# Feature transform in two row tiles, PV in four column tiles, and a new order in an attention, Fourier and feed-forward kernel

## The chip, the cores and the metric

The kernel runs on one core of a Trainium2 chip. The metric is the device time of one execution in microseconds, and the median over runs is compared. The core has TensorE (matmuls, PE in the profile, its weight loads PEld), VectorE (DVE), ScalarE (ACT), GpSimd (POOL) and SyncE (SP), which issues nearly all DMAs here.

## The reference

Inputs are q, k, v of 4 batches, 12 heads, 448 positions and 64 features each, all f32, and two feed-forward weights of 768 x 3072 and 3072 x 768.

```python
scores = scale * np.matmul(q, k.transpose(0, 1, 3, 2))      # causal mask, softmax
attn_out = np.matmul(attn, v)                                # heads side by side: x is (4, 448, 768)
X = np.fft.fft(np.fft.fft(x, axis=1), axis=2)
u = x + np.real(X)
un = (u - mu) / np.sqrt(var + 1e-06)                         # over the 768 features
return u + np.maximum(un @ w_ch1, 0.0) @ w_ch2
```

## The kernel before

Each step of the program is a unit: a small function, the engine that it runs on, what it reads and writes. Four tables in the code fix everything about the units: RUN is the order in which all of them are emitted, BY the engine of each (P for TensorE, V, S, G, and D for a DMA), BANK the PSUM bank and BUF the buffer. The costs that stand beside the units (SC_COST, D1_COST and the like) went into these tables and are not used at run time. Every engine works through its own units in the order of RUN.

Attention (`attend`, lines 539 to 690) goes by pairs of heads, 6 pairs for each batch, 24 in all. Per pair:
- The queries are scaled into qs (L568 on VectorE or GpSimd, L566 on ScalarE).
- The scores are made in three units. Row blocks 0 and 1 share one, row block 2 has another; in both the two heads lie in the two halves of the 128 rows, so that a matmul has 64 rows (L600, and L593 for the mask, bf16 matmuls that add a large number where a key is masked). The third unit is the tail, both heads in one matmul of 128 rows. The masks come first in all three.
- Minimum (L613, VectorE), exponential with its sum (L621, ScalarE), and normalization of seven blocks p (L651 ScalarE, L653 VectorE, L655 GpSimd).
- 16 transposes in four units (L667, f32), copied out of PSUM to pa.
- PV (L677): for each of seven parts and each head one f32 matmul with 64 weight columns, so that the two heads fill two column tiles and the 128 output partitions are the features of two heads. Then two copies to xt, feature by position.

When a pair and its partner three places on are done, `fold` (lines 691 to 717) makes sums and differences of features and of positions, in f0, f1 and f2. `dft` (lines 719 to 842) runs once per batch: per parity of the position and for cosine and sine (nm is a or b) it multiplies by the feature table cd, in two units of three f32 matmuls each, one for the even and one for the odd frequencies, 194 and 192 columns (L735). This is the first step of the transform. Its result is copied to y (ya, yb), multiplied by the position table cs (L752), and added to x (transposes of xt at L778, sums at L788); means and variances, the normalization (L821, L818) and transposes back (L831) follow, and the result goes to DRAM.

The feed-forward part follows: `f1` (L1034) and `window` (L1204), matmuls in f32r on blocks that are split into high and low halves by ScalarE, VectorE and GpSimd. Its first units fill gaps from batch 2's attention on; from some 230 us it runs alone.

At the start, `warm` (lines 491 to 503) runs 11 matmuls on zeros, `consts` (505 to 524) loads identity and mask in f32 and casts them to bf16 (bfc, on VectorE and GpSimd), and the first pair's queries and keys come in four pieces, all issued by SP.

## Time and profile before

| | us |
|---|---|
| median of 3 runs | 850.25 (850.23 to 851.16) |
| the profiled execution | 849.51 |
| its span, first to last instruction | 847.7 |

Shares of the span that the engines are busy: TensorE 99%, its weight loads 89%, VectorE 84%, ScalarE 66%, GpSimd 56%. The profile is one execution. Starts of matmuls are recorded, their ends modelled, and a matmul's recorded duration contains its way through the array: matmuls that follow one another overlap in it. So the distance from one start to the next is what an instruction costs, and the busy share tells only that TensorE never stood for long. A f32 matmul is recorded as two passes, each with its weight load; f32r and bf16 matmuls as one. The chain leads back from the last instruction to what released each step, and merges neighbours of one line. Merged timeline rows run from the first start to the last end.

### The profile page before, as it was taken

What the parts mean: (1) busy time and instruction counts of PE and PEld (TensorE: products, weight loads), DVE (VectorE), ACT (ScalarE), POOL (GpSimd) and SP (SyncE); (2) the same over time, 40 slices, a digit from 0 to 9 for tenths busy, and PEclk for the clock granted to TensorE, in tenths of its full rate; (3) what the DMA queues carried; (4) which work ended last, traced back from release to release, by engine and by line L of the source; (5) the groups of instructions that cost most, each with busy time, mean ns of one, the idle gap of its engine ahead of it and who ended that gap; (6) DMA issues with size and microseconds to landing.
All of it is one profiled execution on the core that took longest, in us unless ns stands there. A gap on an engine that the chain in (4) does not pass through costs nothing.

```text
span 847.7 us, 15801 instructions
## 1 busy us (share of the span) xinstructions
PE 840.2 (99%) x5407; PEld 755.7 (89%) x5407; DVE 711.7 (84%) x1300; ACT 556.2 (66%) x1148; POOL 472.9 (56%) x509
## 2 busy tenths in 40 slices
...
GB/s 270 203 73 201 226 159 237 245 174 165 232 256 212 232 252 298 284 255 255 265 262 250 263 244 235 186 194 208 94 186 188 145 308 143 113 183 143 131 140 102
DMA packets 121792, 174.03 MB, mean 205 GB/s; under 512 B 21744, under 2 KB 98800, under 8 KB 121712
## 3 DMA queue, kind: packets, MB, share of 16 engines
...
## 4 chain that ended last, share of the span: by engine, by line
PE 90%; DVE 4%; DMA 2%; ACT 2%; issue 1%; POOL 0%; SPq 0%; DVEq 0%; ACTq 0%
PE psum L1204 35%; PE psum L1034 31%; PE psum L600 6%; PE psum L677 5%; PE psum L667 5%; PE psum L735 3%; PE psum L593 1%; PE psum L752 1%; PE psum L778 1%; PE psum L831 1%; DMA raw<-in_qk_dram 1%; DMA us<-und 1%; DVE w L896 1%; DMA w<-in_w_dram 0%; DVE us L902 0%
## 5 line engine op out<-in xcount | busy, mean ns | idle before, releaser
L1204 PE MATMUL psum<-wa,w 128*128 128x384 f32 x1050 | 208.3, 336 | 0.0
L1204 PEld LDWEIGHTS psum<-wa,w 128*128 128x128 f32 x1050 | 184.1, 188 | 0.9 <-DVE w L896 0.2
L1204 PE MATMUL psum<-wb,w 128*128 128x384 f32 x714 | 149.7, 337 | 0.2
L1204 PEld LDWEIGHTS psum<-wb,w 128*128 128x128 f32 x714 | 125.8, 188 | 1.3 <-issue 0.4
L1034 PE MATMUL psum<-0t,w 128*128 128x448 f32 x432 | 106.3, 366 | 0.0
L1034 PE MATMUL psum<-1t,w 128*128 128x448 f32 x432 | 103.6, 363 | 0.0
L896 POOL TENSOR_TENSOR w<-ws,w 128x384 fp32r<-128x384 f32 x58 | 67.1, 1162 | 59.6 <-ACT w L487 46.2
L870 ACT ACTIVATE w<-w 128x768 int8<-128x768 f32 x48 | 94.5, 1968 | 0.7
L487 ACT CAST w<-us 128x384 fp32r<-128x384 f32 x77 | 38.5, 513 | 80.9 <-PE psum L1204 34.6
L621 ACT ACTIVATE p<-psum,mn 128x256 f32<-128x256 f32 (+3 forms) x168 | 83.5, 530 | 9.9 <-DVE mn L613 9.3
L1034 PEld LDWEIGHTS psum<-1t,w 128*128 128x128 f32 x432 | 80.7, 187 | 6.2 <-ACT c L487 0.4
L1034 PEld LDWEIGHTS psum<-0t,w 128*128 128x128 f32 x432 | 80.1, 188 | 6.4 <-DVE c L1060 0.4
L487 ACT CAST w<-ws 128x384 fp32r<-128x384 f32 x86 | 44.3, 519 | 47.5 <-PE psum L1204 25.9
L1220 DVE TENSOR_TENSOR acc<-psum,acc 128x384 f32<-128x384 f32 x96 | 50.8, 548 | 23.0 <-PE psum L1204 22.8
L613 DVE TENSOR_REDUCE mn<-psum 128x1 f32<-128x448 f32 (+3 forms) x96 | 61.9, 664 | 6.7 <-PE psum L600 5.0
L600 PE MATMUL psum<-raw,qs 64*128 64x384 f32 (+3 forms) x336 | 66.0, 430 | 1.0 <-DVE qs L568 1.0
L896 POOL TENSOR_TENSOR w<-us,w 128x384 fp32r<-128x384 f32 x40 | 46.9, 1175 | 31.1 <-ACT w L487 16.9
L880 DVE SCALAR_TENSOR_TENSOR w<-w,w 128x768 uint32<-128x768 uint32 x48 | 53.0, 1105 | 3.0 <-ACT w L870 2.4
L1034 PE MATMUL psum<-ue,w 128*128 128x448 f32 x216 | 54.3, 367 | 0.3 <-ACT c L1068 0.3
L1060 DVE TENSOR_TENSOR c<-psum,c 128x448 f32<-128x448 f32 x69 | 42.3, 617 | 13.5 <-PE psum L1034 7.9
L667 PEld LDWEIGHTS psum<-cst,p 128*128 128x128 f32 x384 | 42.7, 141 | 11.1 <-issue 3.9
L655 POOL TENSOR_TENSOR p<-p,ri 128x128 f32<-128x128 f32 (+3 forms) x61 | 37.4, 632 | 26.5 <-DVE ri L633 21.5
...
## 6 DMA issues: line engine op xcount, KB each, us to landing
...
```

The costliest lines, as they stand in the source:

```text
L487: nc.scalar.copy(out=out, in_=in_)
L600: nc.tensor.matmul(out=T[ps][:, at[r]:at[r] + n], lhsT=T[qs][s, q0:q0 + 128], rhs=T[raw][s, QW:QW + n], start=False, stop=y == len(rows) - ...
L613: nc.vector.tensor_reduce(out=z, in_=x, axis=AX, op=ALU.min)
L621: nc.scalar.activation(out=T[pb][:, PO[rr]:PO[rr] + n], in_=T[ps][:, c0:c0 + n], func=ACTF.Exp, scale=-1.0, bias=T[mn][:, rr:rr + 1], accu ...
L667: nc.tensor.transpose(T[ps][:, 128 * k:128 * k + 128], T[pb][:, e:e + 128], T["cst", 0][:, 0:128])
L677: nc.tensor.matmul(out=T[xps][64 * h:64 * h + 64, q0:q0 + w], lhsT=T[v][:, c, h * D:(h + 1) * D], rhs=T[pa][:, s0 + h * sd:s0 + h * sd + w ...
L870: nc.scalar.activation(out=T[w].bitcast(I8)[:, :, 3], in_=T[w][:, :, 1].bitcast(F32), func=ACTF.Prelu, scale=SIGN_SCALE, alpha=SIGN_ALPHA)
L880: nc.vector.scalar_tensor_tensor(out=T[w32], in0=T[w32], scalar=3, in1=T[w][:, :, int(join)], op0=ALU.logical_shift_left, op1=ALU.bitwise_or)
L896: (nc.gpsimd if eng == "G" else nc.vector).tensor_tensor(out=lo(), in0=src(), in1=hi(), op=ALU.subtract)
L1034: nc.tensor.matmul(out=T[ps][:, 0:S], lhsT=w[:, a, t], rhs=T[us[t]][:, b], start=first and k == 0, stop=last and k == 8, skip_group_check= ...
L1204: nc.tensor.matmul(out=T[ps][:, 0:384], lhsT=T[hb][:, a, y], rhs=T[z][:, b], start=first and y + v == 0, stop=last and y == n - 1 and v == ...
L1220: nc.vector.tensor_tensor(out=x, in0=T[ps][:, 0:384], in1=x, op=ALU.add)
```

## The change

- The value columns are permuted on the host so that the even features of both heads come first and then the odd ones. PV issues four matmuls of 32 weight columns for each part instead of two of 64, with a tile position each.
- The output partitions of PV therefore hold even features in the lower and odd ones in the upper half. The first step of the transform takes 97 frequencies for each of two table halves (0 to 96 even, 0 to 95 odd) and runs even and odd features as two matmuls of 64 rows, into two PSUM banks. One bank is copied to yt (ScalarE or VectorE), and VectorE makes the frequencies below the middle as a sum and those above as a difference, in mirrored order. The table is half as large. 385 columns of y are used instead of 386, and the sums with x read and write permuted columns.
- Masks: within a row block the mask of 64 columns now comes before that of 128; for row block 2 the scores come first and the masks last.
- Start: 6 warm-up matmuls instead of 11, their memset on GpSimd; the bf16 constants are prepared on the host, so the casts fall away; the first keys and the masks' constants are issued by ScalarE.
- RUN, BY, BANK and BUF are written anew.

```diff
@@ -38,18 +38,18 @@
 BANKS = dict(sc=(1, 3), sd=(1, 2), pt=(1, 3), x=(1, 2), ay=(1, 3), an=(1, 1), at=(1, 5), h0=(0, 4), h1=(0, 4), o2=(0, 8))
-N_P, N_XT, N_Y, N_F, N_D = 3, 1, 1, 1, 1
+N_P, N_XT, N_Y, N_F, N_D, N_YT = 3, 1, 1, 1, 1, 2
 AFTER = dict(E0=("A1",), E2=("A1", "A2"), L=("Q",), F=("E2",), G=("L",))
 BELOW = dict(E2=("E0",))
-C_FROM, W_FROM, N_WARM = 0, 0, 11
+C_FROM, W_FROM, N_WARM = 0, 0, 6
 N_W1, N_C, N_WS = 8, 3, 3
 N_UB, N_US = 4, 4
-SC_COST, TR_COST, PV_COST = (873, 823, 918), 437, 1816
-D1_COST, D2_COST = 977, 650
+SC_COST, TR_COST, PV_COST = (873, 743, 891), 437, 1830
+D1_COST, D2_COST = 585, 650
 BIG = float(2 ** 30)
@@ -87,298 +87,300 @@
 RUN = (
...
 BY = (
...
 BANK = (
...
 BUF = (
...
...
@@ -493,8 +495,8 @@
         def f():
-            nc.vector.memset(T[z][:, 0, 0:256], 0.0)
-        add("V", 200, -4000, f, wr=[(*z, "warm")], phase="A")
+            nc.gpsimd.memset(T[z][:, 0, 0:256], 0.0)
+        add("G", 150, -4000, f, wr=[(*z, "warm")], phase="A")
@@ -503,15 +505,14 @@
     def consts():
-        for key, c0, c1, p in (("b", 128, CW, -2498.5), ("a", 0, 128, -2300)):
-            def f(c0=c0, c1=c1):
-                nc.sync.dma_start(out=T["cst", 0][:, c0:c1], in_=cc[:, c0:c1])
-            add("D", dma(512 * (c1 - c0)), p, f, wr=[("cst", 0, key)], phase="A")
-
-            def f(eng, c0=c0, c1=c1):
-                copy(eng, T["bfc", 0][:, c0:c1], T["cst", 0][:, c0:c1])
-            n = c1 - c0
-            add(("S", "V", "G"), (acts(n), dve(n, 1.92), gps(n)), p + 600, f, rd=[("cst", 0, key)], wr=[("bfc", 0, key)], phase="A")
+        for key, c0, c1, p in (("b", 64, CW // 2, -2498.5), ("a", 0, 64, -2300.5)):
+            def f(c0=c0, c1=c1, first=key == "b"):
+                (nc.scalar if first else nc.sync).dma_start(out=T["bfc", 0].bitcast(F32)[:, c0:c1], in_=cb[:, c0:c1])
+            add("D", dma(512 * (c1 - c0)), p, f, wr=[("bfc", 0, key)], phase="A")
+
+        def f():
+            nc.sync.dma_start(out=T["cst", 0], in_=cc)
+        add("D", dma(65536), -2300, f, wr=[("cst", 0, "a")], phase="A")
...
@@ -541,16 +542,16 @@
-        def load(c0, c1, keys, p):
+        def load(c0, c1, keys, p, second=False):
             def f():
-                nc.sync.dma_start(out=T[raw][:, c0:c1], in_=qk[b, t][:, c0:c1])
+                (nc.scalar if second else nc.sync).dma_start(out=T[raw][:, c0:c1], in_=qk[b, t][:, c0:c1])
             add("D", dma(512 * (c1 - c0)), p, f, wr=keys, phase="A")
         if i == 0:
-            load(QW, QW + 256, [(*raw, "k")], base - 2500)
+            load(QW, QW + 256, [(*raw, "k")], base - 2500, True)
             load(0, 256, [(*raw, "q")], base - 2499)
             load(256, QW, [(*raw, "q1")], base - 2498)
-            load(QW + 256, QW + S, [(*raw, "k1")], base - 2497)
+            load(QW + 256, QW + S, [(*raw, "k1")], base - 2497, True)
         else:
@@ -581,25 +582,23 @@
                 ones, mask = T["bfc", 0][:, 256:CW], T["bfc", 0][:, 128:256]
+                masks, scores = [], []
                 for y, r in enumerate(rows):
-                    e = at[r] + KE[r]
+                    e, n, q0 = at[r] + KE[r], KE[r], 384 if tail else 128 * r
                     if tail:
-                        moves = [(banks[0], e - 64, 64, T["bfc", 0][:, 0:128], mask)]
+                        masks.append((banks[0], e - 64, 64, T["bfc", 0][:, 0:128], mask[:, 0:64]))
                     else:
-                        moves = [
-                            (ps, e - w, w, ones[64 * h:64 * h + 64, a:a + 128], mask[64 * h:64 * h + 64])
-                            for w, a in ((128, 64), (64, 0)) for h, ps in enumerate(banks)]
-                    for z, (ps, c0, w, a, x) in enumerate(moves):
-                        nc.tensor.matmul(
-                            out=T[ps][:, c0:c0 + w], lhsT=a, rhs=x[:, 0:w], start=y == 0 and z < len(banks), stop=False,
-                            skip_group_check=True)
-                for y, r in enumerate(rows):
-                    n, q0 = KE[r], 384 if tail else 128 * r
+                        masks += [
+                            (ps, e - w, w, ones[64 * h:64 * h + 64, a:a + 128], mask[64 * h:64 * h + 64, 0:w])
+                            for w, a in ((64, 0), (128, 64)) for h, ps in enumerate(banks)]
                     for h, ps in enumerate(banks):
                         s = slice(0, 128) if tail else slice(64 * h, 64 * h + 64)
-                        nc.tensor.matmul(
-                            out=T[ps][:, at[r]:at[r] + n], lhsT=T[qs][s, q0:q0 + 128], rhs=T[raw][s, QW:QW + n],
-                            start=False, stop=y == len(rows) - 1, skip_group_check=True)
+                        scores.append((ps, at[r], n, T[qs][s, q0:q0 + 128], T[raw][s, QW:QW + n]))
+                moves = scores + masks if rows == [2] else masks + scores
+                for z, (ps, c0, w, a, x) in enumerate(moves):
+                    nc.tensor.matmul(
+                        out=T[ps][:, c0:c0 + w], lhsT=a, rhs=x, start=z < len(banks), stop=z >= len(moves) - len(banks),
+                        skip_group_check=True)
             add("PE", SC_COST[0 if tail else len(rows)], p0, f, rd=[*([(*qs, 0), (*raw, "k")] if i or k == 0 else [(*qs, 0), (*qs, 1), (*raw, "k"), (*raw, "k1")]), *([(*raw, "k1")] if i else []),
@@ -673,10 +672,11 @@
             for c, q0, w, s0, sd in PARTS:
-                for h in range(2):
+                for z in range(4):
+                    h = z % 2
                     nc.tensor.matmul(
-                        out=T[xps][64 * h:64 * h + 64, q0:q0 + w], lhsT=T[v][:, c, h * D:(h + 1) * D],
-                        rhs=T[pa][:, s0 + h * sd:s0 + h * sd + w], start=q0 + c == 0, stop=c == 3)
+                        out=T[xps][32 * z:32 * z + 32, q0:q0 + w], lhsT=T[v][:, c, 32 * z:32 * z + 32],
+                        rhs=T[pa][:, s0 + h * sd:s0 + h * sd + w], start=q0 + c == 0, stop=c == 3, tile_position=(0, 32 * z))
         add("PE", PV_COST, base + TR_AT + 700, f, rd=[v, *[(*pa, g) for g in range(4)]], wr=[xps], phase="A", mode="C")
@@ -728,21 +728,36 @@
                 mat = 0 if nm == "a" else 1
-                ps = ("ay", (b, par, nm, 1))
-                for dpar, n0, n1 in ((0, 0, 194), (1, 194, 386)):
-                    def f(c0=c0, w=w, mat=mat, ps=ps, dpar=dpar, n0=n0, n1=n1):
+                pe, po = (("ay", (b, par, nm, z)) for z in (1, 3))
+                for dpar in range(2):
+                    def f(c0=c0, w=w, mat=mat, banks=(pe, po), dpar=dpar):
                         for t in range(3):
-                            nc.tensor.matmul(
-                                out=T[ps][0:w, n0:n1], lhsT=T[f"f{t}", (b, t)][:, dpar, c0:c0 + w],
-                                rhs=T["cd", 0][:, mat, t, n0:n1], start=t == 0, stop=t == 2)
+                            for z, ps in enumerate(banks):
+                                s = slice(64 * z, 64 * z + 64)
+                                nc.tensor.matmul(
+                                    out=T[ps][0:w, 97 * dpar:97 * dpar + 97], lhsT=T[f"f{t}", (b, t)][s, dpar, c0:c0 + w],
+                                    rhs=T["cd", 0][s, mat, t, 97 * dpar:97 * dpar + 97], start=t == 0, stop=t == 2)
                     add("PE", D1_COST, nxt(), f, rd=[*[(f"f{t}", (b, t), g) for t in range(3)], ("cd", 0, mat)],
-                        wr=[(*ps, dpar)], phase="Q")
-                y = ("y" + nm, (b, par))
-                rd = [(*ps, 0), (*ps, 1)]
-
-                def f(eng, w=w, ps=ps, y=y):
-                    copy(eng, T[y][0:w], T[ps][0:w, 0:386])
-                add(("S", "V"), (act(386), dve(386)), nxt(), f, rd=rd, wr=[y], phase="Q")
+                        wr=[(*pe, dpar), (*po, dpar)], phase="Q", mode="H")
+                y, yt = ("y" + nm, (b, par)), ("yt", (b, par, nm))
+
+                def f(eng, w=w, po=po, yt=yt):
+                    copy(eng, T[yt][0:w], T[po][0:w, 0:194])
+                add(("S", "V"), (act(194), dve(194)), nxt(), f, rd=[(*po, 0), (*po, 1)], wr=[yt], phase="Q")
+
+                def two(x, w):
+                    return x[0:w].rearrange("p (o c) -> p o c", o=2)
+
+                def f(w=w, pe=pe, yt=yt, y=y, two=two):
+                    nc.vector.tensor_tensor(
+                        out=two(T[y], w)[:, :, 0:97], in0=two(T[pe][:, 0:194], w), in1=two(T[yt], w), op=ALU.add)
+                add("V", dve(194), nxt(), f, rd=[(*pe, 0), (*pe, 1), yt], wr=[(*y, 0)], phase="Q")
+
+                def f(w=w, pe=pe, yt=yt, y=y, two=two, mat=mat):
+                    x = [two(z, w)[:, :, 0:96][:, :, ::-1] for z in (T[pe][:, 0:194], T[yt])]
+                    nc.vector.tensor_tensor(
+                        out=two(T[y][:, 1:385], w)[:, :, 96:192], in0=x[mat], in1=x[1 - mat], op=ALU.subtract)
+                add("V", dve(192), nxt(), f, rd=[(*pe, 0), (*pe, 1), yt, (*y, 0)], wr=[(*y, 1)], phase="Q")
             for nm, g in (("b", 2 + par), ("a", par)):
@@ -750,17 +765,17 @@
                     nc.tensor.matmul(
-                        out=T[ps][0:m, 0:386], lhsT=T["cs", 0][0:k, g, 0:m], rhs=T[y][0:k], start=True, stop=True)
-                add("PE", D2_COST, nxt(), f, rd=[y, ("cs", 0, 0)], wr=[ps], phase="Q")
+                        out=T[ps][0:m, 0:385], lhsT=T["cs", 0][0:k, g, 0:m], rhs=T[y][0:k, 0:385], start=True, stop=True)
+                add("PE", D2_COST, nxt(), f, rd=[(*y, 1), ("cs", 0, 0)], wr=[ps], phase="Q")
                 if nm == "b":
                     def f(eng, m=m, ps=ps, bs=bs):
-                        copy(eng, T[bs][0:m], T[ps][0:m, 0:386])
+                        copy(eng, T[bs][0:m, 0:385], T[ps][0:m, 0:385])
                     add(("S", "V"), (act(386), dve(386)), pr[0] + 1, f, rd=[ps], wr=[bs], phase="Q")
                             nc.vector.tensor_tensor(
-                                out=T[z, (b, par)][0:m, 0:386], in0=T[ps][0:m, 0:386], in1=T[bs][0:m], op=op)
+                                out=T[z, (b, par)][0:m, 0:385], in0=T[ps][0:m, 0:385], in1=T[bs][0:m, 0:385], op=op)
                         add("V", dve(386), pr[0] + 1, f, rd=[ps, bs], wr=[(z, (b, par))], phase="Q")
@@ -781,13 +796,12 @@
                     def f(hf=hf, w=w, ps=ps, key=key, u=u):
-                        if hf:
-                            z = T[key][0:w, 0:386].rearrange("p (o c) -> p c o", o=2)[:, ::-1][:, 0:192]
-                        else:
-                            z = T[key][0:w].rearrange("p (o c) -> p c o", o=2)[:, 0:192]
+                        z = T[key][0:w, hf:hf + (384 if hf else 386)].rearrange("p (o c) -> p o c", o=2)
+                        z = z[:, :, ::-1] if hf else z[:, :, 0:192]
                         nc.vector.tensor_tensor(
-                            out=T[u][0:w, 384 * hf:384 * hf + 384].rearrange("p (c o) -> p c o", o=2),
-                            in0=T[ps][0:w, 0:384].rearrange("p (c o) -> p c o", o=2), in1=z, op=ALU.add)
+                            out=T[u][0:w, 384 * hf:384 * hf + 384].rearrange("p (t i o) -> p o t i", t=3, o=2),
+                            in0=T[ps][0:w, 0:384].rearrange("p (t o i) -> p o t i", t=3, o=2),
+                            in1=z.rearrange("p o (t i) -> p o t i", t=3), op=ALU.add)
                     add("V", dve(384), pr[0] + 1, f, rd=[ps, key], wr=[(*u, hf)], phase="Q")
@@ -1339,17 +1353,12 @@
 def _tables():
-    d = np.arange(384)
-    cd = np.zeros((2, 3, 128, 386), np.float64)
-    even, odd = 2 * np.arange(193), 2 * np.arange(192) + 1
-    for m, f in ((0, np.cos), (1, np.sin)):
-        full = np.zeros((384, 386))
-        full[:, 0:193] = f(2 * np.pi * ((d[:, None] * even[None, :]) % DM) / DM)
-        full[:, 194:386] = f(2 * np.pi * ((d[:, None] * odd[None, :]) % DM) / DM)
-        if m == 1:
-            full[:, 0] = 0.0
-            full[:, 192] = 0.0
-        cd[m] = full.reshape(3, 128, 386)
+    p = np.arange(128)
+    d = 128 * np.arange(3)[:, None] + 2 * (p % 64) + p // 64
+    freq = np.concatenate([2 * np.arange(97), 2 * np.arange(96) + 1])
+    cd = np.zeros((2, 3, 128, 194), np.float64)
+    cd[:, :, :, 0:193] = [f(2 * np.pi * ((d[:, :, None] * freq) % DM) / DM) for f in (np.cos, np.sin)]
+    cd[1, :, :, 0] = 0.0
     cs = np.zeros((4, 128, 113), np.float64)
...
@@ -1372,9 +1381,9 @@
     cd, cs = _tables()
-    mask = np.concatenate(
-        [np.tile(np.triu(np.ones((64, 64)), 1), (2, 1)) * BIG, np.full((128, 64), BIG), np.zeros((128, 64)),
-         np.tile(np.eye(64), (2, 1)), np.zeros((128, 64))], axis=1)
+    bits = np.concatenate(
+        [np.eye(128), np.tile(np.triu(np.ones((64, 64)), 1), (2, 1)) * BIG, np.full((128, 64), BIG), np.zeros((128, 64)),
+         np.tile(np.eye(64), (2, 1)), np.zeros((128, 64))], axis=1).astype(np.float32).view(np.uint32) >> 16
@@ -1384,7 +1393,7 @@
     vpad = np.zeros((B, NP, 512, 128), np.float32)
-    vv = inputs["v"].reshape(B, NP, 2, S, D).transpose(0, 1, 3, 2, 4).reshape(B, NP, S, 128)
+    vv = inputs["v"].reshape(B, NP, 2, S, D // 2, 2).transpose(0, 1, 3, 5, 2, 4).reshape(B, NP, S, 128)
     vpad[:, :, :384], vpad[:, :, 448:] = vv[:, :, :384], vv[:, :, 384:]
@@ -1393,7 +1402,8 @@
         "w2": inputs["moe_w_ch2"].reshape(2 * NCH, 128, DM),
-        "cc": np.concatenate([np.eye(128), mask], axis=1).astype(np.float32),
+        "cc": np.eye(128).astype(np.float32),
+        "cb": bits.astype(np.uint16).view(np.float32),
         "cd": cd,
```

## Rows read from the trace of the kernel before

**Rows 1.** The page, parts 1 and 4: TensorE's busy time; the chain by engine.

```profile
PE 840.2 (99%) x5407; PEld 755.7 (89%) x5407; DVE 711.7 (84%) x1300; ACT 556.2 (66%) x1148; POOL 472.9 (56%) x509
...
PE 90%; DVE 4%; DMA 2%; ACT 2%; issue 1%; POOL 0%; SPq 0%; DVEq 0%; ACTq 0%
```

**Rows 2.** Chain in order of time, 50 to 70: start us, duration us, what.

```profile
53.10 0.73 PE psum L600 x4
...
54.74 1.91 PE psum L677 x28
...
65.67 0.44 PE psum L667 x4
...
66.44 0.98 PE psum L735 x6
```

**Rows 3.** Windows: stretch, length; busy PE, PEld, DVE, ACT, POOL; PEclk, DMA, GB/s.

```profile
0.00:230.00 230.00, 227.00 (x2115) 169.69 (x2116) 202.10 (x436) 207.41 (x584) 132.70 (x207) 1.00 0.61 196
80.00:140.00 60.00, 59.86 (x562) 44.85 (x558) 56.87 (x122) 59.46 (x158) 42.23 (x67) 1.00 0.66 219
230.00:290.00 60.00, 59.13 (x302) 51.42 (x301) 57.06 (x108) 53.34 (x93) 23.73 (x32) 1.00 0.73 231
290.00:510.00 220.00, 219.96 (x1097) 204.77 (x1095) 176.37 (x307) 157.36 (x212) 93.65 (x84) 1.00 0.79 263
```

**Rows 4.** Instructions of one line, L735 then L600: weight loads, ns min/median/max.

```profile
L735 PEld LDWEIGHTS psum<-cd,f x192: 172/176/178, 57.1 to 231.0; 128*112 128x112 f32 x96, 128*111 128x111 f32 x48, 128*113 128x113 f32 x48
...
L600 PEld LDWEIGHTS psum<-raw,qs x336: 184/188/201, 5.7 to 203.3; 64*128 64x128 f32 x144, 128*128 128x128 f32 x24
```

**Rows 5.** Timeline, weight loads from 22.02 and 22.13 on: start us, duration us.

```profile
22.02 0.30 PEld L600 LDWEIGHTS psum<-raw,qs 64*128 64x128 f32 x4
...
22.13 0.30 PEld L600 LDWEIGHTS psum<-raw,qs 64*128 64x128 f32 x4
```

**Rows 6.** Timeline of TensorE in narrow windows between 21.4 and 23.6 us.

```profile
21.44 0.38 PE L667 MATMUL psum<-cst,p 128*128 128x128 f32 x2
...
21.76 0.34 PE L593 MATMUL psum<-bfc 64*128 64x128 bf16 x8
21.94 0.36 PE L600 MATMUL psum<-raw,qs 64*128 64x128 f32 x2
...
22.76 0.57 PE L600 MATMUL psum<-raw,qs 64*128 64x384 f32 x2
...
23.17 0.48 PE L600 MATMUL psum<-raw,qs 64*128 64x384 f32 x2
```

**Rows 7.** Timeline of TensorE, two narrow windows at the end of one PV.

```profile
25.07 0.40 PE L677 MATMUL psum<-pa,v 128*64 128x64 f32 x8
...
25.07 0.46 PE L677 MATMUL psum<-pa,v 128*64 128x64 f32 x10
```

**Rows 8.** Timeline of the start; in brackets idle time before, and releaser.

```profile
1.17 4.45 PE L502 MATMUL psum<-xt 128*128 128x512 bf16 x11 [1.17 <-DVE xt L496]
1.57 0.15 PEld L502 LDWEIGHTS <-xt 128*128 128x128 bf16 x1 [0.28 <-issue]
2.00 0.15 PEld L502 LDWEIGHTS <-xt 128*128 128x128 bf16 x1 [0.28 <-issue]
...
3.52 1.38 SPq L546 DMA_DIRECT2D raw<-in_qk_dram  x3
...
5.55 0.34 PE L593 MATMUL psum<-bfc 64*128 64x128 bf16 x8
...
9.43 1.02 PE L600 MATMUL psum<-raw,qs 128*128 128x448 f32 x2 [0.98 <-DVE qs L568]
```

**Rows 9.** Groups by line up to 240 us: count, busy us, mean ns.

```profile
L489 DVE COPY pa<-psum 128x512 f32<-128x512 f32 x39 | 25.7, 677 | 2.2 <-PE psum L667 0.8 <-PE psum L593 0.5 <-issue 0.5
...
L714 DVE TENSOR_TENSOR f<-o 128x222 f32<-128x222 f32 x5 | 1.9, 386 | 0.0
...
L655 POOL TENSOR_TENSOR p<-p,ri 128x128 f32<-128x128 f32 (+3 forms) x61 | 37.4, 632 | 26.5 <-DVE ri L633 21.5 <-ACT xt L487 1.5 <-ACT pa L487 1.5
```

126 lines of the change are left out of this document (63 added, 63 removed), and 460 rows, old and new, of the table RUN.

## The prediction

> **What bounds the kernel now.** I read the page's busy part and its chain first [rows 1]: TensorE is busy 99% of the span and carries 90% of the chain. Matmul ends are modelled there, so I looked next at how far apart the matmuls start. In the chain in order of time [rows 2] long blocks run at a fixed pitch: 6 passes of the feature transform (L735) in 0.98 us, 0.163 us each, and 4 transposes in 0.44 us. So TensorE is full of work, and a part that gets shorter there moves the end, provided that the others keep up. The windows [rows 3] tell whether they do: up to 230 us VectorE is busy 202.1 us and ScalarE 207.4 us, up to 290 us (with the next window) VectorE has 259.2 us (89%) and ScalarE 260.8 us (90%); from 290 to 510 us only 80% and 72%. The change edits the first 230 us alone; the feed-forward work behind (L1034, L1204) keeps its instructions. I take the whole gain or loss as TensorE's, and ask at the end if VectorE lets it through.
>
> **The feature transform (lines 731 to 738).** Before: 192 passes (a f32 matmul is recorded as two) over 128 rows and 192 or 194 columns [rows 4], at 0.163 us [rows 2]: 31.3 us. After: the even and the odd features lie in the two halves of the rows, each pass has 97 columns and 64 rows, and two of them are meant to run side by side: 192 pairs of passes. That f32 passes of 64 rows do run side by side is in the trace: the scores of row block 2 are 4 passes of 384 columns in 0.73 us [rows 2]; at the pace of the transform (0.163 us for 193 columns, 0.84 ns each) they would take 1.29 us one after the other. What is the pitch of a pair? The stream gives 97 x 0.84 = 0.082 us. But weights must be loaded for each pass, and their columns (111 to 113) are not halved. In the scores, loads of 128 columns for successive pairs start at 22.02 and 22.13 [rows 5], 0.11 us apart. A load there has 188 ns, in the transform 172 to 178 [rows 4], 12 less: 0.098 us. I take 0.098 (the load, not the stream, sets it), with 0.082 and 0.111 as ends: 18.8 us after (15.7 to 21.3), a gain of 12.5 us (10.0 to 15.6). The Trainium skill, page "TensorE: Matmul & The Clock Gate", Part 2, section LDWEIGHTS, says that a load's time goes by its columns and not its rows, columns divided by 1.2 per ns. It speaks against half of what the halving promises; by it a pair would take 0.093 us (an estimate) and the transform 17.9 us, the gain 13.4 instead of 12.5 us.
>
> **Changes of form.** Units over 64 rows (scores), over 128 rows, and over column tiles (PV) follow each other; where the form changes, time is lost: the last transpose starts at 21.55 (the second of the two from 21.44) and the masks at 21.76, 0.21 us where transposes stand 0.11 us apart [rows 6, 2]. So 0.10 us each. Going through RUN and taking TensorE's units in turn, before has 89 changes, after 104: +1.5 us. 23 of the 32 transform units after stand behind another 64-row unit; for the 9 others the first load is not hidden: 9 x 0.09 = 0.8 us.
>
> **Masks last, and the short mask first.** In row block 2 the second pair of score passes starts 0.41 us after the first (22.76 to 23.17) [rows 6], though 384 columns stream in 0.32: the load of its f32 weights isn't hidden by the short mask in front. With the scores first it is hidden where the unit before has 64 rows too: 15 of 24 by RUN, 15 x 0.085 = 1.3 us; in the other 9 the long load then stands ahead, and I take nothing. In row blocks 0 and 1 the last mask ahead of the scores gets 128 columns instead of 64. The 384 columns of masks per half take 0.18 us (21.76 to 21.94) [rows 6], 0.47 ns each, so it hides 0.03 us more of the load: 24 x 0.03 = 0.7 us. Together 2.0 us (ends: nothing, and 2.7 if all 24 gain).
>
> **PV in four column tiles.** 28 passes per pair of heads become 56 of half the width, over the same columns; 1.91 us per unit now [rows 2]. Two column tiles run side by side already: at the end of a PV, two more passes of 64 columns lengthen it by 0.06 us [rows 7], the stream of one. The trace has no four. Below: no cost, since the streams are the same. Above: if the four need twice the time in the 8 narrow groups, 8 x 0.05 = 0.4 us per unit, 10 us in all. I take the lower end, nearest to the row of two tiles, with an allowance of 0.3 us in all for twice the starts, and keep 10 as a rival.
>
> **The start.** Eleven warm-up matmuls start from 1.17 on, 0.43 us apart (loads at 1.57 and 2.00) [rows 8]: 512 columns in that time is the 1.2 GHz level, although the clock column prints 1.00. Scores begin at 5.55, right behind the last. Six end at about 1.17 + 6 x 0.43 = 3.8. The first keys and the masks, now in bf16 and without a cast on VectorE, are issued by ScalarE beside SP; SP issues fewer transfers ahead of the second pair's load, at 3.52 now [rows 8], for which TensorE stands 0.98 us at 9.43. First scores should come some 1.5 us sooner, partly at 1.2 GHz: I take 1.2 us, between 2.0 sooner and 1.0 later (if the clock rises late). The memset goes from VectorE to GpSimd, which has nothing else yet; the table load on ScalarE falls behind its three issues, hidden as ScalarE still waits for the first scores' minima then. Smaller constant tables and 385 for 386 columns: nothing.
>
> **The sum.** -12.5 + 1.5 + 0.8 - 2.0 + 0.3 - 1.2 = -13.1 us. The span of 847.7 becomes 834.6; the profiled execution took 849.5, 1.8 more, and the median of the runs, 850.25, lies 0.74 over that: 837.2 us.
>
> **Does VectorE let it through?** The 16 copies of 386 columns become 16 of 194 and 32 additions on VectorE; with 0.38 us each, as a sum of 222 columns has [rows 9], 12.2 us. By BY, VectorE loses five copies of pa (0.68 us each [rows 9]), four of xt, two of the transform, three normalizations and two scalings, some 7.6 us with the two short copies that it gets instead: 12.2 - 7.6 = 4.6 us more. ScalarE loses eleven normalizations and takes over those copies, so it has no more to do than now. GpSimd gets 14 normalizations more, 0.63 us each [rows 9], and is busy 133 of 230 us [rows 3]. VectorE would then need 263.8 of 278 us, 95%. It holds that today: from 80 to 140 us it is 95% busy and ScalarE 99% while TensorE is at 59.9 of 60 us [rows 3]; and preparation of later weights can slip past 290 us, where there is room. In a new order stalls can come and go; TensorE's own idle time is 847.7 - 840.2 = 7.5 us now [rows 1], so I expect little either way.
>
> **Rivals.**
> - VectorE lets part of it through. If it gets to 92.5% instead of 95%, the first 290 us shrink by 5, not 13: 845 us. For it: two additions in place of one copy, where it is busiest already. Against: the 95% stretch. 13%.
> - VectorE stays at its 89%: 263.8 / 0.894 = 295 us for what takes 290 now, 855 us, slower than before. It decides once VectorE holds less than 91% (263.8 of 290). Against: the same stretch, and that later work can be put off. 6%.
> - PV is held up by its starts: four narrow passes need 0.10 us, not 0.05: 837.2 + 9.6 - 0.3 = 846.5. For it: in the masks 8 matmuls start in 0.18 us, 0.022 each [rows 6], and here 0.013 would be wanted. Against: those were bound by streams and loads. 6%. The Trainium skill, same page, Part 1 ("Wait - 56ns, not 53.3ns?"), says starts never come closer than about 25 ns; by that a group of four would need 0.1 us (an estimate). Masks at 0.022 us for two tiles speak against such a floor across tiles.
> - Four f32 column tiles run two by two: PV doubles its stream (1024 columns, two passes, 0.84 ns each: 1.7 us), 24 x 1.7 = 41 us, 878 us. Against: two tiles overlap fully. 3%.
> - More is gained: pairs at 0.082 us, the start 2 us sooner, stalls gone: 829 to 833. 7%.
>
> **How the numbers follow.** The forecast, 833 to 841, has 65%. Range 832 to 846: it takes in the ends of the transform, the start, PV's starts and most of the partial case. A measurement of this kernel can tell about 0.2% (1.7 us) from no change. Slower: 6 + 3%. Same: 2%, from the edge of the partial case. Faster: the other 89%.
>
> **What would show it.** L735: 384 passes, pairs 0.098 us apart, the two of a pair starting within some ns. 0.082 would make the load wrong, over 0.13 the overlap. PV blocks of 56 in 1.92 us, else one of its two rivals. The second pair of row block 2 at 0.32 us, not 0.41. First scores near 4 us. VectorE near 95% up to the point where L1034 runs alone, which should come 12 us sooner; if TensorE's waits on VectorE or ScalarE grow by several us there, the first rival is right. A changed pitch in L1034 or L1204 would upset the whole sum.

## The result and the profile after

The changed kernel takes 841.59 us (median of 4 runs, 840.55 to 842.77) where the kernel before took 850.24 on the same chip: a ratio of 0.990, with an interval of 0.989 to 0.991, 8.65 us less. 13.1 had been forecast. The profiled execution took 840.55 us with a span of 838.8, 8.9 less than before. So the question of this study is where 4 us went.

The page after, busy time and chain by engine, answers to [rows 1]:

```profile
PE 828.2 (99%) x6266; PEld 745.5 (89%) x6266; DVE 721.4 (86%) x1324; ACT 555.1 (66%) x1146; POOL 473.8 (56%) x517
...
PE 81%; DVE 9%; ACT 6%; issue 2%; DMA 1%; POOL 0%; SPq 0%; DVEq 0%; ACTq 0%; POOLq 0%
```

TensorE is still called 99% busy, but its part of the chain has fallen from 90 to 81%, and VectorE and ScalarE have 15% instead of 6. The chain in order of time (start us, duration us, what) shows the edited blocks, as [rows 2] did:

```profile
53.51 1.88 PE psum L677 x56
55.39 1.36 PE psum L737 x24
...
61.87 2.53 PE psum L737 x48
```

The transform's first step is now L737: 48 passes, 24 pairs, in 2.53 us with the changes of form before and behind them. PV's 56 matmuls take 1.88 us, where 28 took 1.91. The line of the first step by itself (weight loads and matmuls, ns min/median/max), beside [rows 4]:

```profile
L737 PEld LDWEIGHTS psum<-cd,f x384: 168/175/176, 55.3 to 223.6; 64*112 64x112 f32 x96, 64*111 64x111 f32 x49, 64*113 64x113 f32 x47
L737 PE MATMUL psum<-cd,f x384: 257/258/336, 55.3 to 223.7; 64*112 64x97 f32 x96, 64*111 64x97 f32 x49, 64*113 64x97 f32 x47
```

A load of half the rows takes 175 ns, as long as one of all rows (176). Windows (stretch, length; busy PE, PEld, DVE, ACT, POOL; PEclk, DMA, GB/s), as [rows 3], and at the end two longer stretches, the second of which the experiments use:

```profile
0.00:230.00 230.00, 223.68 (x3005) 163.59 (x3006) 208.63 (x458) 211.85 (x592) 150.06 (x230) 1.00 0.64 202
80.00:140.00 60.00, 58.10 (x824) 42.36 (x824) 57.64 (x130) 57.94 (x156) 43.48 (x69) 1.00 0.70 230
230.00:290.00 60.00, 59.52 (x311) 54.28 (x310) 58.82 (x113) 55.16 (x95) 19.97 (x27) 1.00 0.76 239
290.00:510.00 220.00, 219.68 (x1097) 204.92 (x1096) 183.37 (x310) 157.70 (x213) 90.39 (x79) 1.00 0.79 260
...
0.00:290.00 290.00, 283.20 (x3314) 217.87 (x3315) 267.45 (x570) 267.01 (x686) 170.03 (x256) 1.00 0.66 210
...
40.00:290.00 250.00, 245.37 (x2844) 192.65 (x2842) 237.22 (x506) 234.60 (x579) 147.99 (x221) 1.00 0.67 211
```

VectorE is busy 95% of the time from 40 to 290 us, where the kernel before had 92% (its row stands with e1). The prediction counted from the start, though, and there VectorE reaches 92.2% (267.45 of 290 us) after 89.4% [rows 3], not the 95% that was wanted. TensorE is busy 58.10 of 60 us from 80 to 140, where it had been 59.86. What it waits for between 12 and 250 us (waiting line, what ended the wait, us in total, times, longest), first before, then after:

```profile
PE psum L752 <- ACT ya L487: 0.4, 1, 0.4
PE psum L677 <- ACT pa L487: 0.2, 1, 0.2
```

```profile
PE psum L737 <- ACT p L620: 0.9, 2, 0.6
PE psum L767 <- DVE yb L758: 0.6, 1, 0.6
PE psum L767 <- ACT bs L489: 0.6, 1, 0.6
PE psum L677 <- ACT pa L489: 0.4, 1, 0.4
PE psum L737 <- DVE f L714: 0.4, 1, 0.4
PE psum L845 <- ACT un L832: 0.3, 1, 0.3
PE psum L666 <- ACT pa L489: 0.2, 1, 0.2
PE psum L793 <- DVE yb L758: 0.2, 1, 0.2
PE psum L599 <- ACT xt L489: 0.2, 1, 0.2
PE psum L793 <- ACT p L620: 0.2, 1, 0.2
```

0.6 us in two waits have become 4.0 in eleven. Two kinds are mixed here. Some waits are for an input: the position step L767 for the difference yb (L758), PV for pa, L737 for f, L845 for un, 1.7 us together. The others can't be, since the waiting line doesn't read what ended them: L737 does not read p, nor L666 pa, nor L793 yb. These events are the last reading of a PSUM bank that TensorE is to write next: 0.9 + 0.6 + 4 x 0.2 = 2.3 us. Before, both waits were for an input.

This view lists the larger waits only. Reckoned over all units (from a unit's start to the next one's, less the shortest such stretch among units of its kind with the same forms around it; each excess put down to the last event among its inputs and the readers of its bank), TensorE's waits from 12 to 250 us are 8.1 us before and 14.5 after, and those ended by a reader of the bank 1.1 and 6.7. I call this the unit reckoning below; its classes are inferred and its sums are rough (the account below comes out some 2 us short of the measured gain with them), and the listed waits stand beside it where they decide.

The start (start us, us, engine, line; in brackets idle time and what ended it), beside [rows 8]:

```profile
1.08 2.74 PE L504 MATMUL psum<-xt 128*128 128x512 bf16 x6 [1.08 <-POOL eps L518]
3.76 0.50 PE L599 MATMUL psum<-bfc 64*128 64x64 bf16 x8
4.17 1.65 PE L599 MATMUL psum<-raw,qs 64*128 64x128 f32 x8
6.82 0.92 PE L599 MATMUL psum<-raw,qs 64*128 64x384 f32 x4 [0.99 <-DMA raw<-in_qk_dram]
12.86 1.97 PE L666 MATMUL psum<-cst,p 128*128 128x128 f32 x16
```

Scores begin at 3.76 us, as forecast, but the first eight passes take 1.65 us where later ones of the kind take 0.88 to 0.90: nearly twice, as the 1.2 GHz level would give, though the clock column prints 1.00 there. (It varies: in the profiled execution of e9, with the same start, they take 0.94.) Then row block 2 stands for 0.99 us until the second half of the keys lands. The first transposes start at 12.86, where the kernel before had 13.39 in its profiled execution.

### The profile page after: what moved, and what is told of

It reads as the page before. It is cut to its first block, busy times and chain, and to the rows that moved or that the text cites. A ratio compares the mean times of both kernels' runs of the same rounds, so it can differ in the third digit from the quotient of the medians.

```text
span 838.8 us, 17526 instructions
## 1 busy us (share of the span) xinstructions
PE 828.2 (99%) x6266; PEld 745.5 (89%) x6266; DVE 721.4 (86%) x1324; ACT 555.1 (66%) x1146; POOL 473.8 (56%) x517
## 4 chain that ended last, share of the span: by engine, by line
PE 81%; DVE 9%; ACT 6%; issue 2%; DMA 1%; POOL 0%; SPq 0%; DVEq 0%; ACTq 0%; POOLq 0%
PE psum L1218 36%; PE psum L1048 32%; PE psum L599 3%; PE psum L666 3%; PE psum L677 3%; ACT p L620 3%; DVE mn L612 1%; PE psum L737 1%; PE psum L767 1%; ACT pa L489 1%; DVE w L894 1%; ACT p L650 1%; DVE w L910 1%; PE psum L793 1%; DMA raw<-in_qk_dram 1%
## 5 line engine op out<-in xcount | busy, mean ns | idle before, releaser
L910 POOL TENSOR_TENSOR w<-ws,w 128x384 fp32r<-128x384 f32 x57 | 69.0, 1212 | 59.0 <-ACT w L489 34.3
L620 ACT ACTIVATE p<-psum,mn 128x384 f32<-128x384 f32 (+3 forms) x168 | 83.0, 506 | 6.5 <-DVE mn L612 5.6
L489 ACT CAST w<-us 128x384 fp32r<-128x384 f32 x70 | 35.6, 514 | 66.3 <-PE psum L1218 25.9
L599 PE MATMUL psum<-raw,qs 64*128 64x256 f32 (+3 forms) x336 | 65.1, 427 | 1.4 <-DMA raw<-in_qk_dram 1.0
L654 POOL TENSOR_TENSOR p<-p,ri 128x128 f32<-128x128 f32 (+3 forms) x75 | 46.4, 639 | 20.3 <-DVE ri L632 13.6
L489 ACT CAST w<-c 128x384 fp32r<-128x384 f32 x44 | 22.4, 514 | 48.8 <-PE psum L1218 27.9
L910 POOL TENSOR_TENSOR w<-us,w 128x384 fp32r<-128x384 f32 x37 | 43.4, 1177 | 19.4 <-ACT w L489 10.3
L894 DVE SCALAR_TENSOR_TENSOR w<-w,w 128x768 uint32<-128x768 uint32 x48 | 50.3, 1047 | 3.5 <-ACT w L884 2.2
L666 PEld LDWEIGHTS psum<-cst,p 128*128 128x128 f32 x384 | 42.5, 141 | 10.2 <-issue 4.1
```

The lines of the kernel that those rows point to most:

```text
L489: nc.scalar.copy(out=out, in_=in_)
L599: nc.tensor.matmul(out=T[ps][:, c0:c0 + w], lhsT=a, rhs=x, start=z < len(banks), stop=z >= len(moves) - len(banks), skip_group_check=True)
L620: nc.scalar.activation(out=T[pb][:, PO[rr]:PO[rr] + n], in_=T[ps][:, c0:c0 + n], func=ACTF.Exp, scale=-1.0, bias=T[mn][:, rr:rr + 1], accu ...
L654: nc.gpsimd.tensor_tensor(out=x, in0=x, in1=z.to_broadcast([128, KE[r]]), op=ALU.mult)
L666: nc.tensor.transpose(T[ps][:, 128 * k:128 * k + 128], T[pb][:, e:e + 128], T["cst", 0][:, 0:128])
L894: nc.vector.scalar_tensor_tensor(out=T[w32], in0=T[w32], scalar=3, in1=T[w][:, :, int(join)], op0=ALU.logical_shift_left, op1=ALU.bitwise_or)
```

## The experiments

Four theories were put to the test. A: VectorE, or VectorE and ScalarE, have too much to do (the prediction's first rival). B: the way from the first step to the position step has become longer, copy, sum and difference instead of one copy. C: the new order itself costs. E came later, when C and A had failed: the first step's second output bank makes the eight banks tight. Each kernel was timed beside the kernel before on the same chip; times of different groups are compared by their ratio to it (a difference of 0.001 is 0.85 us, and the ends of an interval are some 0.0015 off its middle).

| run | ratio to before | interval | against its base, us |
|---|---|---|---|
| changed kernel | 0.9902 | 0.989 to 0.991 | -8.3 (before) |
| e1, transform undone | 1.0008 | 1.000 to 1.002 | +9.0 (changed) |
| e2, short chain | 0.9894 | 0.988 to 0.991 | -0.7 (changed) |
| e3, no clamp | 0.9871 | 0.986 to 0.989 | -2.6 (changed) |
| e4, before without clamp | 0.9974 | 0.996 to 0.998 | -2.2 (before) |
| e5, order of before | 1.0153 | 1.014 to 1.017 | +21.3 (changed) |
| e6, k1 by SyncE | 0.9907 | 0.989 to 0.993 | +0.4 (changed) |
| e7, before with masks last | 0.9997 | 0.999 to 1.001 | -0.3 (before) |
| e8, banks dealt anew | 0.9907 | 0.989 to 0.992 | +0.4 (changed) |
| e9, no clamp, no sign | 0.9872 | 0.985 to 0.989 | -2.6 (changed) |
| e10, before with neither | 0.9969 | 0.996 to 0.998 | -2.6 (before) |
| e11, e1 with its spare bank | 0.9965 | 0.995 to 0.998 | -3.7 (e1) |
| e12, shared banks | 0.9932 | 0.992 to 0.995 | +2.6 (changed) |

**e1: the transform's first step undone.**

```diff
-                            for z, ps in enumerate(banks):
-                                s = slice(64 * z, 64 * z + 64)
-                                nc.tensor.matmul(
-                                    out=T[ps][0:w, 97 * dpar:97 * dpar + 97], lhsT=T[f"f{t}", (b, t)][s, dpar, c0:c0 + w],
-                                    rhs=T["cd", 0][s, mat, t, 97 * dpar:97 * dpar + 97], start=t == 0, stop=t == 2)
+                            nc.tensor.matmul(
+                                out=T[banks[0]][0:w, n0:n1], lhsT=T[f"f{t}", (b, t)][:, dpar, c0:c0 + w],
+                                rhs=T["cd", 0][:, mat, t, n0:n1], start=t == 0, stop=t == 2)
```

> The changed kernel with its transform's first step as it was: six passes over all 128 rows, 193 or 192 columns, into one bank, one copy of 385 columns where the copy of 194 stood, no additions; order, PV, masks and start of the changed kernel stay. By the trace of after, 32 units of 0.64 us (0.585 and a form change in about every second) become 32 of 0.975: +10.7 us of TensorE. Theory A (VectorE's and ScalarE's load makes TensorE wait): 5.6 us of VectorE's work go (32 additions of 0.35, less half of that in the copies' growth on ScalarE), so some 4 us of waits go with it: near 848. Theory B (the longer chain from the transform's end through copy, sum and difference to the position step is what TensorE waits for): the same, near 848, since the chain is gone. Theory C (the new order of the work is what costs, whatever the transform's form): the waits stay and the whole 10.7 comes back, 852.

Measured: 850.2 us, 1.0008 of before, between the two expectations. By the unit reckoning the waits did not fall (14.0 us), although the chain was short again and VectorE had less to do than before the change. The window from 40 to 290 us, e1 and then the kernel before:

```profile
40.00:290.00 250.00, 246.10 (x2608) 195.55 (x2607) 221.09 (x460) 228.73 (x570) 142.65 (x219) 1.00 0.63 201
```

```profile
40.00:290.00 250.00, 248.43 (x2060) 197.10 (x2059) 230.11 (x479) 227.33 (x570) 138.15 (x205) 1.00 0.63 198
```

VectorE is busy 221.1 us for 230.1, and TensorE waits more. At that point this spoke for C.

**e2: a shorter chain.**

```diff
-                        out=two(T[y][:, 1:385], w)[:, :, 96:192], in0=x[mat], in1=x[1 - mat], op=ALU.subtract)
+                        out=x[1], in0=x[mat], in1=x[1 - mat], op=ALU.subtract)
...
+                    z = T[y][0:k].rearrange("p (o c) -> p o c", o=2)[:, :, 0:97].unsqueeze(2).to_broadcast([k, 2, 2, 97])
...
-                        out=T[ps][0:m, 0:385], lhsT=T["cs", 0][0:k, g, 0:m], rhs=T[y][0:k, 0:385], start=True, stop=True)
-                add("PE", D2_COST, nxt(), f, rd=[(*y, 1), ("cs", 0, 0)], wr=[ps], phase="Q")
+                        out=T[ps][0:m, 0:388], lhsT=T["cs", 0][0:k, g, 0:m], rhs=z, start=True, stop=True)
+                add("PE", D2_COST, nxt(), f, rd=[(*y, 0), ("cs", 0, 0)], wr=[ps], phase="Q")
```

> The changed kernel, but the position step waits for the sum alone: the difference is computed, as long as before, into the copy's buffer, where nobody reads it, and the position step reads the sum's columns twice (388 columns for 385). The feature transform's second half of frequencies is so left out. VectorE does as much as before. Theory A (load): within 0.5 us of the changed kernel, 841 to 842. Theory B (length of the chain): the position steps start about 0.4 us sooner where they waited; of the 3.9 us that they and the 2.5 us that the first steps wait, 2 to 3 us go: 838.5 to 839.5. Theory C: no change.

Measured: 0.7 us less, which can't be told from nothing. One operation less in the chain is worth little in the new order.

**e3, e4, e9, e10: less load.** The clamp of the weights is left out (e3, e4), or the clamp and the instruction of the sign (e9, e10), in the changed kernel and in the one before.

```diff
-            nc.vector.tensor_scalar(out=x, in0=x, scalar1=W_TOP, scalar2=None, op0=ALU.min)
+            pass
...
-                nc.scalar.activation(
-                    out=T[w].bitcast(I8)[:, :, 3], in_=T[w][:, :, 1].bitcast(F32), func=ACTF.Prelu, scale=SIGN_SCALE, alpha=SIGN_ALPHA)
+                pass
```

> The changed kernel without the minimum that clamps the dequantized weights: 48 VectorE instructions of 0.6 us (4 of them in each pair of chunks), some 10 us of them before 245 us. Theory A (VectorE's load): VectorE falls from 95% to about 91% in 40 to 290 us and the extra waits of TensorE (17 us before f1, against 9 in the kernel before) fall by 3 to 5 us: 837 to 838.5. Theory B: the chain's length stays, at most 1 us gained: 840.5. Theory C: at most 1 us.

> The kernel before with the same instructions left out. It had VectorE at 89 to 92% in the stretch and TensorE's waits before f1 at 9 us. Theory A: VectorE was not yet the limit there, so it gains less than the changed kernel does, 0 to 1.5 us: 848.7 to 850.2. Theories B and C: as little as the changed kernel gains, 0 to 1 us. If it gains as much as the changed kernel, then VectorE's load held both alike, and does not account for the missing part.

> The changed kernel without the clamp and without the ScalarE instruction that puts the weights' sign byte in place: between 20 and 245 us 5.9 us of VectorE's and 17.8 us of ScalarE's work less, in all 48 of each. Theory A in its wider form (VectorE and ScalarE together are too full, either alone doesn't help): TensorE's waits before f1 fall from 17 us to 11 or less; by the first f1 stretch, at 290 us, the work is 4 to 6 us sooner than in the changed kernel, against 2.1 without the clamp alone. If the waits are of distance (a copy, a sum and a difference that must pass between two steps of TensorE that stand close together, or a bank that must be read out): the waits stay at 14 us or more, and the work is at most 3 us sooner at 290 us.

> The kernel before without the same two instructions. Wider theory A: it has 9 us of TensorE's waits before f1 and loses at most 2 to 3 of them: 1.5 to 3 us sooner at 290 us, less than the changed kernel by 2 us or more. Distance: as much sooner as the changed kernel, to 1 us.

Measured: 2.6 and 2.2 us without the clamp, 2.6 and 2.6 without both. e3 alone would have met theory A's number; beside e4 it says nothing for A, since the kernel before gains as much. e9's window shows how much was taken away, to be read beside the last row of the windows above:

```profile
40.00:290.00 250.00, 246.76 (x2855) 195.30 (x2854) 232.58 (x497) 215.52 (x571) 148.81 (x222) 1.00 0.66 213
```

ScalarE has 215.5 instead of 234.6 us, VectorE 232.6 instead of 237.2, and TensorE's largest waits are:

```profile
PE psum L737 <- ACT p L620: 0.9, 2, 0.6
PE psum L767 <- ACT bs L489: 0.6, 1, 0.6
PE psum L677 <- DVE ri L632: 0.4, 1, 0.4
...
```

The first two lines are those of the changed kernel, to the tenth: waits that don't move when 24 us of work (19.1 and 4.6) go from two engines are not waits for those engines' load. Others did move. The position step's wait for the difference yb (0.6) is no longer listed, and the listed waits sum to 2.7 us instead of 4.0, while in the kernel before they went from 0.6 to 1.1.

By whole times, and at 290 us, where the expectations had set the test (TensorE reaches the same unit 2.6 us sooner in e9 and 2.1 in e10), theory A falls as the account of the whole, in the wider form too. It does not fall as a part. Counted from the first transposes, the unit that TensorE starts at 250 us comes 1.0 us sooner in e3 and 1.8 in e9, but in the kernel before 0.4 sooner in e4 and 0.2 later in e10; that kernel gains only behind, in the feed-forward work. Each has one profile, and e2 and e6, which leave the load as it was, moved by 0.6 and 0.1 us between the same two points. So 1 to 2 us of TensorE's waits ahead of 250 us may be load; more is not shown.

**e5: all of the change in the order of the kernel before.** RUN and BY are those of before, each unit in its counterpart's place; copy, sum and difference stand where the copy stood.

```diff
 RUN = (
-    0, 8, 2, 5, 7, 9, 1, 10, 3, 48, 94, 4, 49, 11, 132, 12, 14, 13, 6, 21, 18, 15, 25, 17, 20, 50, 131, 19, 22, 54,
+    0, 8, 5, 7, 9, 6, 10, 1, 3, 4, 48, 94, 131, 95, 132, 11, 12, 2, 14, 13, 21, 18, 25, 20, 22, 19, 50, 24, 15, 51,
...
```

> All of the change's parts, but the work of every engine in the order of the kernel before: each unit stands where its counterpart stood, the copy's place takes copy, sum and difference; the two first-step units of a transform stand together, and the PSUM banks are dealt anew, since the transform takes two. Which engine does a copy or a normalisation is as before, too. Undisturbed, TensorE's work is the changed kernel's. Theory C (the new order is what costs: with the transform undone in that order 19 us of TensorE's waits stayed, against 9 in the kernel before, at VectorE's old load): waits fall back to about 10, and the time to 834 to 837. Theory B (the longer chain costs): in this order, where the position step stood one copy behind the transform, it now stands copy, sum and difference behind it: waits of 15 us or more, 841 to 845. Theory A (VectorE's load): VectorE has the same work as in the changed kernel, so about its 841.

Measured: 862.6 us, 13 more than the kernel before. Theory C falls with it: the old order is far worse for the new work. The largest waits (line numbers are 288 smaller in this kernel, as its tables stand on one line each: L479 is the position step, L470 the difference, L449 the first step, L378 the transposes, L201 the copy on ScalarE):

```profile
PE psum L479 <- DVE ya L470: 2.3, 3, 1.2
PE psum L479 <- ACT 0t L201: 2.3, 1, 2.3
PE psum L449 <- ACT xt L201: 2.2, 2, 1.2
PE psum L378 <- ACT p L362: 1.5, 2, 1.3
PE psum L378 <- DVE st L520: 1.0, 1, 1.0
PE psum L505 <- ACT bs L201: 0.9, 1, 0.9
...
```

The position step waits for the difference, up to 1.2 us at a time, and the first step for a bank (it doesn't read xt). The listed waits, of which these are the largest, sum to some 14 us; the start, which the new order also serves, is 2.6 us later (first transposes at 15.47). So theory B is right in part in this order: the waits for a difference (ya, yb) sum to 2.9 us, and the 2.3 us put down to 0t may be a third kind of them, since they end 0.14 us behind another difference. Most of the others are for a bank. The new order hides such waits, and what the chain alone costs is not told by this run: the banks were dealt anew here, who normalizes is as before too, there are 113 changes of form instead of 104, and TensorE's clock is granted at 0.50 for two stretches of together 6.8 us, from 178.9 and 236.9 us, the first 2 us behind a wait of 1.2 us, the second within the wait of 2.3. All four executions have a mean granted clock of 0.995 or 0.996, where the changed kernel has 1.000.

**e6: the second half of the first keys by SyncE.**

```diff
-            load(QW + 256, QW + S, [(*raw, "k1")], base - 2497, True)
+            load(QW + 256, QW + S, [(*raw, "k1")], base - 2497)
```

> The changed kernel, but the second half of the first keys (96 KB, issued by ScalarE at 1.7 us and landing 5 us later, in front of row block 2's scores, which waited 1 us for it) is issued by SyncE again, behind the first queries and keys. If the queue it is on makes it late, it lands about 1 us sooner and the first transposes come up to 1 us sooner: 840 to 840.6. If the sum of the first loads makes it late, whichever queue carries them, no change: 841.

Measured: no change in the time. Its profiled execution had no wait in front of row block 2 and its first transposes at 11.96; but seven executions with the changed kernel's start (after, e1, e2, e3, e8, e9, e11) have them anywhere from 12.27 to 12.91, and e12, which has SyncE too, at 12.70. In e6's trace the 0.9 us that the start gained still stand at 510 us and are down to 0.2 at the end, so under 1 us the end of a run tells little. Whether the queue matters stays open.

**e7: the masks alone, in the kernel before.**

```diff
+                moves = scores + masks if rows == [2] else masks + scores
```

> The kernel before with one part of the change: the masks of row block 2 behind its scores. By the trace of after, a row block 2 behind a 64-row unit starts its scores' first pass without the form change inside (0.823 to 0.730 us), and the others keep theirs; the order has 7 to 12 of the 24 units behind such a unit: 0.6 to 1.1 us, less what goes in waits: 848.3 to 849 where the kernel before has 849.4.

Measured: 0.3 us less, in an interval of 0.8 to either side; the expected 0.6 to 1.1 is neither confirmed nor excluded as a time. The blocks do show it: the 12 units of row block 2 that stand behind 64 rows go from 0.906 to 0.824 us, the other 12 get 0.014 longer, 0.8 us in all.

**e8: the banks dealt anew.** Same work, same order; BANK alone is changed, so that a bank rests longer between its last reader and its next writer.

```diff
 BANK = (
-    "41267035147245671631202345014010345640277756344560531256071324054042552722237062063730507367125026746734465673"
+    "16745042511312672542203467316540456763157023674063401234731564605236506630227047074251525567125041302367527037"
...
```

> The changed kernel with the same work in the same order, but its PSUM banks dealt anew up to f1, so that a bank is written again later after its last reader (248 of some 500 uses moved to another bank; in the changed kernel the transform's first step at 167.3 us and the position step at 219.5 us each waited 0.6 us for a reader of their bank, and 2.3 of the 4.0 us of listed waits between 20 and 245 us ended with such a reader). Theory E (the transform's second bank makes all banks tight, and that is what TensorE waits for): 1.5 to 2.3 us gained, 838.5 to 839.5. Theory A (load of VectorE and ScalarE) and theory B (the chain's length): the waits end with another event on the same engines, at most 0.5 us: 840.5 to 841.

Measured: no change. By the unit reckoning the waits on a bank's reader fell from 6.7 to 4.0 us, and others rose by as much. Dealing eight full banks in another way moves the waits about.

**e11: e1 with the spare bank given back.** e1 had kept out of the deal a second bank for each first step that nothing used. Here BANK is dealt without it, in the manner of e8.

```diff
 BANK = (
-    "41267035147245671631202345014010345640277756344560531256071324054042552722237062063730507367125026746734465673"
+    "16701335147245671631202345172430345601463056123705074512274313044274643740507363006721227612343042756756542075"
...
```

> As the run with the transform's first step undone (six passes of 128 rows into one bank; new order, PV, masks and start kept; 850.2 us, 1.001 of the kernel before), but the second bank of each pair, which that run no longer used and yet kept out of the deal, goes back to the others, and the banks are dealt anew for it. By each wait's last event, TensorE's waits between 12 and 250 us that ended with a reader of the bank it was to write were 1.1 us in the kernel before, 6.7 in the changed kernel and 8.2 in that run. Theory E (the pair's second bank, not the chain or the load, is what TensorE waits for): these waits fall to 2 to 5 us, the time by 3 to 5: 845 to 847. If the new order as such holds them, whatever the banks: 849 to 850.5.

Measured: 847.2 us, 0.9965 against e1's 1.0008: 3.7 us less by the ratios, with the two intervals apart, and 2.8 in the profiled spans (848.5 to 845.7), of which 0.6 lie ahead of the first transposes. The largest four of e1's ten listed waits:

```profile
PE psum L666 <- DVE ub L491: 0.8, 1, 0.8
PE psum L763 <- ACT bs L489: 0.6, 1, 0.6
PE psum L677 <- ACT pa L489: 0.4, 1, 0.4
PE psum L666 <- DVE pa L491: 0.3, 1, 0.3
...
```

All that are listed in e11:

```profile
PE psum L677 <- ACT pa L489: 0.7, 1, 0.7
PE psum L841 <- ACT un L828: 0.4, 1, 0.4
PE psum L736 <- DVE f L714: 0.3, 1, 0.3
PE psum L1044 <- ACT c L489: 0.2, 1, 0.2
```

The transposes' waits on readers of their bank (ub, pa) are gone, so is the position step's on bs; PV's wait for its input pa stays. By the unit reckoning, waits on a bank's reader fell from 8.2 to 3.3 us. Theory E holds here, at the lower end of what was expected; and since e8 dealt in the same manner and gained nothing, it is likely the freed bank and not the dealing (e1 with a new deal and the bank kept out was not run). In the stretch that the banks serve the gain is larger: e11 starts the same unit 4.8 us sooner than e1 at 250 us, start included, and 2.7 at 290. Between, VectorE is busy for all of 260 to 270 us and TensorE for 9.4 of the 10: the waits listed there are for the feed-forward inputs c and w, so part of what the banks give back is lost again to that preparation.

**e12: two first steps in one pair of banks.** In the changed kernel the sine and the cosine step share their banks, BANK is dealt for it, and k1 comes by SyncE.

```diff
-                pe, po = (("ay", (b, par, nm, z)) for z in (1, 3))
+                pe, po = (("ay", (b, par, z)) for z in (1, 3))
+                x0 = 0 if nm == "b" else 256
...
-                                    out=T[ps][0:w, 97 * dpar:97 * dpar + 97], lhsT=T[f"f{t}", (b, t)][s, dpar, c0:c0 + w],
+                                    out=T[ps][0:w, x0 + 97 * dpar:x0 + 97 * dpar + 97], lhsT=T[f"f{t}", (b, t)][s, dpar, c0:c0 + w],
```

> The changed kernel with less need of banks: the sine and the cosine part of a transform (units b and a), which had two banks each for their first steps, share two, one in columns 0 to 193 and one in 256 to 449, and the banks are dealt anew. The second half of the first keys is issued by SyncE, too, which brought the work 0.9 us forward by 26 us and kept 0.9 at 290 us. Theory E: of the 6.7 us of waits on a bank's reader 2 to 4 go beside the start's 0.9: the first f1 stretch, at 290 us, is 3 to 5 us sooner than in the changed kernel, 836.5 to 838.5 in all. If distance or the order hold the waits, whatever the banks: 0.9 sooner at 290 us, 840 to 841.

Measured: 844.2 us, 2.6 more than the changed kernel. Three of the six executions have a mean granted clock of 0.997 or 0.998 and take 844.7 to 845.2 us, the three at 1.000 take 842.0 to 843.7, so about half of the 2.6 goes with the clock; still nothing is gained where 3 to 5 us were expected. Of the waits on a bank's last reader, 2.3 us in the changed kernel, 0.3 are still listed, and a new one has taken their place (line numbers are 1 larger: L738 is the first step, L753 the sum, L759 the difference):

```profile
PE psum L738 <- DVE ya L759: 0.9, 1, 0.9
PE psum L738 <- DVE yb L753: 0.8, 1, 0.8
PE psum L738 <- DVE yt L491: 0.8, 1, 0.8
PE psum L738 <- DVE yb L759: 0.7, 1, 0.7
...
PE psum L738 <- ACT yt L489: 0.6, 2, 0.4
```

3.8 us: in this program the second first step doesn't write its columns until the copy, the sum and the difference of the first have read theirs in the same bank. Sharing a bank put a chain between two steps that had been free of each other.

## Why the prediction was right, and where it was off

The direction was right and the time lies in the range, 4 us above the forecast and 0.6 above the narrower band (833 to 841). That the blocks and the start sum to the forecast's 13.1 us again, as shown below, is partly luck: PV came out 1.0 us better than reckoned, which makes up for the masks (0.3) and the start (0.7). By its steps:

- **The transform: right.** A unit of 12 passes, 6 pairs, takes 0.585 us where no form changes (0.975 before), 0.0975 us a pair against the forecast 0.098. With a change behind it, it takes 0.686 (10 of the 32), and 0.666 where it stands behind a unit without 64 rows (9 of them): 13 x 0.585 + 10 x 0.686 + 9 x 0.666 = 20.5 us for 31.2 before (32 x 0.975), 10.7 less; the terms of the forecast, 12.5 - 1.5 - 0.8, give 10.2. The load sets the pitch, as was argued from [rows 4, 5]. The Trainium skill, page "TensorE: Matmul & The Clock Gate", Part 2, section LDWEIGHTS, has the load's time go by columns and not by rows; the rows agree (175 ns for 64 rows, 176 for 128), and its 0.093 us for a pair, an estimate, is a little short of the 0.0975 seen.
- **Changes of form and masks: right.** Row block 2 behind another score unit of 64 rows went from 0.907 to 0.823 us where PV follows and nothing is waited for; taken for all 15 that stand behind 64 rows that is 1.2 us, though the one behind a transform unit takes 0.931 and gains nothing. The other 9 got 0.014 longer, and the units of row blocks 0 and 1 went from 0.917 to 0.891 (24): 1.2 - 0.1 + 0.6 = 1.7 us at most for a forecast 2.0. The second pair of score passes starts 0.32 us after the first, as forecast. That is read from block lengths; as a time e7 could not show it.
- **PV: wrong sign, small.** 1.88 us for 1.91, 24 x 0.03 = 0.7 us gained where 0.3 was allowed as a cost. Both PV rivals are out.
- **The start: too large by 0.4 to 0.7.** In the profiled pair the first transposes gained 0.53 us, not 1.2. Over the executions that keep these two starts (seven from 12.27 to 12.91, mean 12.53; four, the kernel before, e4, e7 and e10, from 13.08 to 13.86, mean 13.36) it is 0.83. The scores started on time; the lower level of the clock and the late keys, both named as a possible loss, took part of it back.
- **Stalls: this step failed.** The prediction took them as "little either way", on the ground that TensorE's idle time was small and that VectorE could hold 95%. VectorE held 95% from 40 us on, 92.2% as the prediction counted, and got more work than reckoned (711.7 us over the whole run [rows 1] became 721.4, 9.7 more, where 4.6 had been reckoned for the attention and the transform). The listed waits rose by 3.4 us (0.6 to 4.0), the unit reckoning by 6.4. Summed, the blocks and the start give -10.7 - 1.7 - 0.7 - 0.5, and 0.5 for those five of the 15 new changes of form that are not in the first of these, -13.1; with the listed waits -9.7, with the unit reckoning -6.7, and the span says -8.9.
- **The first rival: out as the account of the whole, open as a part.** Its share came about: VectorE is busy 92.2% of the first 290 us, where the rival said 92.5. Its price, 8 of the 13 us, did not. The sign that was named for it, "if TensorE's waits on VectorE or ScalarE grow by several us", was badly chosen: they grew, but the last event before a wait names the engine that ran last, not that it was short of time, and more than half of the listed waits (2.3 of 4.0 us) are for a bank. In e9 and e10 24 us less work for the two engines buys the changed kernel no more than the kernel before by the whole time, and 1 to 2 us more up to 250 us.

What the prediction didn't look at is the PSUM banks. The change has each first step write two banks where it wrote one, and keeps one of them until copy, sum and difference are done, where it was free after the copy. With e11 the account goes so: everything but the transform, with the banks free, is worth 0.0035 of the time, 3.0 us (2.0 by the spans), and masks, PV and start in the account above are 1.7 + 0.7 + 0.5. The transform on top of that brings 5.4 us (0.9965 to 0.9902; 6.9 by the spans) of its 10.7. Of the 5.3 that are missing by the ratios, e1 against e11 lays 2.2 (spans, less the start) to 3.7 (ratios) on the second bank's place in the deal, and e2 some 0.7, not clear of noise, on the difference in the chain. That is shown for the kernel with the transform undone; in the changed kernel itself neither another deal (e8) nor shared banks (e12) gave the time back, so that the same size there is inferred from waits of the same kind (2.3 us of the listed 4.0), not measured. How the rest divides between banks, chain and load is open.

No kernel here that does all of the work is faster than the changed one: e6 and e8 equal it within the interval.
